# One list scheduler for all engines behind the front, one pool of PSUM banks, and another form of the second layer's seven products

## The chip, the cores and the metric

The kernel runs on one core of a Trainium2 chip. The metric is the device time of one execution in microseconds (us); where several executions were timed, their median stands. A core has a matrix engine (TensorE, PE in the profile, whose weight loads have a row of their own, PEld), VectorE (DVE), ScalarE (ACT), GpSimd (POOL) and SyncE (SP). They run side by side, each takes its own instructions strictly in the order in which the program lists them, and semaphores hold an instruction back until its inputs are there. DMAs that POOL or SP issue run on 16 DMA engines.

## The reference

Chunked attention is followed by two dense layers with a leaky ReLU between them:

```python
q_c, k_c, v_c = (t.reshape(B, H, nc, 64, D) for t in (q, k, v))     # B=8, H=8, S=576, D=64
scores = (1 / sqrt(D)) * matmul(q_c, k_c.transpose(0, 1, 2, 4, 3))  # within chunks of 64 tokens
attn = exp(scores - max(scores)); attn = attn / (sum(attn) + 1e-9)
x = matmul(attn, v_c)                       # as 4608 tokens x 512
h = x @ w_in                                # 512 x 2048
g = maximum(0.01 * h, h)
out = g @ w_out                             # 2048 x 512
```

## The kernel before

**Attention, by groups.** The 4608 tokens are 36 groups of 128 (two chunks of 64). Here a group is called u, from 0 to 35. Its way is: `load_qk` (POOL issues the DMAs that load q and k and cast them to fp16; lines 57 to 77); a transposition of both, by TensorE for the groups 0 to 8 (`stage_tq`, `stage_tk`), by DMA from SP for the later ones (`stage_t`, line 567, tiles QT and KT); `stage_p` on POOL (line 576), which spreads QT into the zero-filled tile QZ; `stage_s` (scores, eight small matmuls on TensorE, line 583, tile Sp); on VectorE and ScalarE the maximum, the subtraction, the exponential, the sum, its reciprocal and the product (lines 593, 598, 605, 612 to 616, 622; tiles mx, sh, ex, z, en); a transposition of the probabilities, by SP's DMA from group 9 on (`stage_d`, line 644, tile et); `stage_v` (eight small matmuls with the values VB, line 657, tile xp); `stage_a` (ScalarE copies xp into xT, line 673). xT is a ring of 1536 tokens. V is loaded for one batch (4.5 groups) at a time into two buffers, `load_v`, line 82.

**The two layers, by blocks.** The tokens are cut into blocks of 128 (six), 256 (one) and 512 (seven, the blocks 7 to 13). The first layer, `mm1` (line 171), makes one PSUM bank at a time, 512 columns of hT, which `act1` (line 191) writes to gT with the leaky ReLU. For the blocks 0 to 6 the second layer is plain (`mm2`, line 203). For the seven large blocks it is one step of a Strassen scheme (`product`, line 298): gT and w_out are each cut in 2 x 2 parts, five sums of gT parts are formed on VectorE (`form`, line 263, tiles S and gT), five sums of weights once (`weight_form`, line 234, tile WF), and seven products of half size replace eight. A product is two passes (p = 0, 1) of eight matmuls of 256 columns. The products go to three banks a, b, c; three ScalarE copies (`evict`) and five VectorE sums (`combine`, lines 334 to 343) turn them into the output tile osb, which SP stores. For the last block the same is done by halves (`piece`).

**What sets the order.** The front, up to the transpositions of q and k of group 5, is a list written by hand (`FRONT`). Behind it a loop over rounds `it` issues the attention of some groups, and `fill` puts pieces of the layers between them: five or six pieces of eight matmuls in a round, picked by `pick` with due times that `on` keeps. A group's scores are issued in one round and its `stage_v` three rounds later. In a round POOL's `stage_p` of group u comes ahead of the load of group u + 7, and SP's transpositions of group u + 3 behind the transposition of the probabilities. The layers use the PSUM banks mm0 to mm3 in turn (three of them from block 7 on); attention has the four banks qp, kp, Sp and ox, of which the products share two.

Of the kernel before, what the change touches and what calls it, by code (L numbers as in the profile page):

```python
# [16 lines left out]
def kernel(  # L17
# [9 lines left out]
    nc = tc.nc  # L27
# [12 lines left out]
    NIN = 9  # L40
# [6 lines left out]
    SUB = {7: 128, **{j: 256 for j in range(8, 14)}}  # L47
    RING = 1536
    HB, HM = NFC // 2, d_model // 2

# [10 lines left out]
    WF = sbp.tile([128, 5, HB, HM], FP16, name="WF")  # L61
# [45 lines left out]
    for eng, name, src in ((nc.sync, "q_f", q), (nc.scalar, "k_f", k)):  # L107
        t = sbp.tile([128, H, D], FP32, name=name, tag=name, bufs=1)
        eng.dma_start(out=t, in_=src[0, :, 0:G, :].rearrange("h p d -> p h d"))
        first.append(t)  # L110
# [8 lines left out]
        "g1 v0 g2 Q0 Q1 g3 Q2 Q3 g4 P0 P1 P2 P3 g5 v1 g6 g7 g8 "  # L119
# [8 lines left out]
    gT: dict[int, bass.AP] = {}  # L128
    GT: dict[int, tuple[int, bass.AP]] = {}

    def tile_of(j):

        return START[j] // 512

    START = [sum(BLOCKS[:j]) for j in range(len(BLOCKS))]
    mm_n = {"n": 0, "of": 4}

    def mm_tile(shape, name):

        i = mm_n["n"] % mm_n["of"]  # L140
        mm_n["n"] += 1
        return psp.tile(shape, FP32, name=name, tag=f"mm{i}", bufs=1)


    T = {"pe": 0.0, "dve": 0.0, "act": 0.0}

    def on(engine, us, after=0.0):
        T[engine] = max(T[engine], after) + us
        return T[engine]

    UNIT = 0.87
    when: dict[tuple, float] = {}

    HT: dict[tuple[int, int, int], bass.AP] = {}
    parts: dict[tuple[int, int], int] = {}
    oP: dict[tuple[int, int], bass.AP] = {}
    made: dict[int, int] = {}
    read = {"tokens": 0}
# [4 lines left out]
    def mm1(j, a, h=0):  # L163
# [3 lines left out]
        hT = mm_tile([128, nf, tb], "hT")  # L167
# [10 lines left out]
        on("pe", UNIT)  # L178
        HT[j, a, h] = hT
        made[j] = made.get(j, 0) + 1  # L180
        if made[j] == NFC * BLOCKS[j] // 512:
            read["tokens"] = START[j] + BLOCKS[j]

    def act1(j, a, h=0):
        tb = sub(j)
        nf = 512 // tb
        n = tile_of(j)
        if n not in GT:
            GT[n] = START[j], sbp.tile([128, NFC, 512], FP16, name="gT", tag="gT", bufs=2)
        gT[j] = GT[n][1][:, :, START[j] - GT[n][0]:START[j] - GT[n][0] + BLOCKS[j]]  # L190
        nc.scalar.activation(  # L191
            out=gT[j][:, nf * a:nf * a + nf, h * tb:h * tb + tb], in_=HT.pop((j, a, h)),
            func=AFT.Prelu, bias=0.0, scale=1.0, alpha=0.01,
        )
        when["gT", j] = on("act", 0.62, T["pe"] + 0.2)

    def mm2(j, ti, part):
        n = parts.get((j, ti), 0)
        if n == 0:
            oP[j, ti] = mm_tile([128, d_model], "oP")  # L200
        o = oP[j, ti]
        for fc in range(part * 4, part * 4 + 4):
            nc.tensor.matmul(  # L203
                out=o,
                lhsT=gT[j][:, fc, ti * 128:(ti + 1) * 128],
                rhs=w_outT[:, fc, :],
                start=(n == 0 and fc == part * 4),
                stop=(n == NFC // 4 - 1 and fc == part * 4 + 3),
            )
        on("pe", UNIT)  # L210
        parts[j, ti] = n + 1

    def store(j, ti):
        osb = sbp.tile([128, d_model], FP32, name="osb", tag="osb", bufs=3, padded_shape=[128, 2 * d_model])
        nc.scalar.activation(out=osb, in_=oP.pop((j, ti)), func=AFT.Copy, bias=0.0, scale=1.0)
        on("act", 0.62, T["pe"] + 0.2)
        r0 = START[j] + ti * 128
        nc.sync.dma_start(out=out[r0:r0 + 128, :], in_=osb)

# [4 lines left out]
    WFORMS = (  # L227
        (B12, B22, ALU.subtract), (B21, B11, ALU.subtract), (B11, B22, ALU.add), (B11, B12, ALU.add),
        (B21, B22, ALU.add),
    )  # L230

    def weight_form(i):
        of, by, op = WFORMS[i]
        nc.vector.tensor_tensor(out=WF[:, i], in0=of, in1=by, op=op)
        on("dve", 1.24)

    SF: dict[int, dict[str, bass.AP]] = {}
    BANK: dict[str, bass.AP] = {}
    TMP: dict[str, bass.AP] = {}
    OSB: dict[tuple[int, int], bass.AP] = {}  # L240

    def half_tokens(j):
        return BLOCKS[j] // 2

    def form(j, name):

        if name in SF.setdefault(j, {}):
            return
        for earlier in FORMS[:FORMS.index(name)]:
            form(j, earlier)  # L250
        g, n = gT[j], half_tokens(j)
        a11, a12 = g[:, :HB, :n], g[:, HB:, :n]
        a21, a22 = g[:, :HB, n:2 * n], g[:, HB:, n:2 * n]
        of, by, op, to = {
            "S2": (a21, a22, ALU.add, None),
            "S1": (a11, a22, ALU.add, None),
            "S5": (a11, a12, ALU.add, None),
            "S6": (a21, a11, ALU.subtract, a21),
            "S7": (a12, a22, ALU.subtract, a12),
        }[name]  # L260
        if to is None:
            to = sbp.tile([128, HB, n], FP16, name=name, tag=name, bufs=1, padded_shape=[128, HB, 256])
        nc.vector.tensor_tensor(out=to, in0=of, in1=by, op=op)  # L263
        SF[j][name] = to
        when[name, j] = on("dve", 0.17 + n / 240, when["gT", j])

    FORMS = ("S2", "S1", "S5", "S6", "S7")
    TAGS = {"a": "qp", "b": "kp", "c": "mm3"}

    LAST = len(BLOCKS) - 1  # L270
    ENDS: dict[tuple[str, int], bass.AP] = {}

    def product(j, m, p):
        g, n = gT[j], half_tokens(j)
        if m not in (3, 4):
            form(j, f"S{m}")
        if m == 3:
            lhs, rhs, bank = g[:, :HB, :n], WF[:, 0], "a"
        elif m == 2:
            lhs, rhs, bank = SF[j]["S2"], B11, "b"  # L280
        elif m == 1:
            lhs, rhs, bank = SF[j]["S1"], WF[:, 2], "c"
        elif m == 4:
            lhs, rhs, bank = g[:, HB:, n:2 * n], WF[:, 1], "b"
        elif m == 5:
            lhs, rhs, bank = SF[j]["S5"], B22, "a"
        elif m == 6:
            lhs, rhs, bank = SF[j]["S6"], WF[:, 3], "c"
        else:
            lhs, rhs, bank = SF[j]["S7"], WF[:, 4], "b"  # L290
        opens = m in (1, 2, 3)
        if opens and j == LAST:
            ENDS[bank, p] = psp.tile([128, HM], FP32, name=f"m{bank}", tag=(TAGS[bank], f"mm{'abc'.index(bank)}")[p], bufs=1)
        elif opens and p == 0:
            mm_n["of"] = 3
            BANK[bank] = psp.tile([128, n // 128, HM], FP32, name=f"m{bank}", tag=TAGS[bank], bufs=1)
# [118 lines left out]
    for j in range(PLAIN):  # L415
        chunks += c1(j) + c2(j)
# [407 lines left out]
```

## Time and profile before

| what | value |
|---|---|
| median of 3 runs | 290.98 us (287.64 to 291.55) |
| span of the profiled execution, its own time | 290.3 us |
| PE busy | 274.7 us, 95% |
| PEld busy | 236.7 us, 82% |
| DVE busy | 202.3 us, 70% |
| ACT busy | 149.4 us, 51% |
| POOL busy | 134.0 us, 46% |
| read and written in HBM | 36.70 and 9.44 MB |

The page tells of one execution: busy time by engine, the span in 40 slices with a digit for the busy share in tenths, the DMA queues, the chain of work that ended last, the costliest groups of instructions, and the DMA issues with the time to their landing. Matmul records overlap: a first-layer matmul of 256 columns is listed with 273 ns, but 24 of them take 2.62 us in the chain. The granted TensorE clock is 1.00 throughout.

### The profile page before, as it was taken

What the parts mean: (1) busy time and instruction counts of PE and PEld (TensorE: products, weight loads), DVE (VectorE), ACT (ScalarE), POOL (GpSimd) and SP (SyncE); (2) the same over time, 40 slices, a digit from 0 to 9 for tenths busy, and PEclk for the clock granted to TensorE, in tenths of its full rate; (3) what the DMA queues carried; (4) which work ended last, traced back from release to release, by engine and by line L of the source; (5) the groups of instructions that cost most, each with busy time, mean ns of one, the idle gap of its engine ahead of it and who ended that gap; (6) DMA issues with size and microseconds to landing.
All of it is one profiled execution on the core that took longest, in us unless ns stands there. A gap on an engine that the chain in (4) does not pass through costs nothing.

```text
span 290.3 us, 7618 instructions
## 1 busy us (share of the span) xinstructions
PE 274.7 (95%) x3188; PEld 236.7 (82%) x3188; DVE 202.3 (70%) x332; ACT 149.4 (51%) x263; POOL 134.0 (46%) x166
## 2 busy tenths in 40 slices
PE   4969999999999989999989699999999999999995
PEld 4859945877859978898869599999899998888884
DVE  6987516798875697868987688879788830820292
ACT  6346724655727736465545455556655554534320
POOL 8846647876496336967643798532150000000000
PEclk9999999999999999999999999999999999999999
DMA  9999999999999999999999999999944201200213
GB/s 131 170 191 172 193 162 197 145 163 169 150 145 163 174 124 130 154 124 187 161 147 156 149 229 164 136 155 179 174 62 125 76 2 65 82 0 2 101 66 126
DMA packets 165795, 39.18 MB, mean 135 GB/s; under 512 B 156800, under 2 KB 161408, under 8 KB 165760
## 3 DMA queue, kind: packets, MB, share of 16 engines
q0 software_dynamic: 114336, 18.09, 91.1%
q1 hardware_dynamic: 50384, 20.33, 43.3%
q8 instruction: 25, 0.41, 0.6%
q10 hardware_dynamic: 1040, 0.26, 0.4%
q14 instruction: 10, 0.08, 0.1%
HBM read 36.70 MB, written 9.44 MB: 159 GB/s over the span
## 4 chain that ended last, share of the span: by engine, by line
PE 51%; DMA 35%; POOL 8%; issue 3%; DVE 1%; ACT 0%; POOLq 0%
PE hT L171 22%; DMA q_in<-in_q_dram 19%; DMA k_in<-in_k_dram 10%; PE mb L298 9%; PE oP L203 6%; PE mc L298 5%; PE ma L298 5%; DMA w_inT<-in_moe_w_in_dram 4%; DMA et<-en 3%; POOL VB L82 3%; POOL QZ L576 2%; POOL k_in L73 2%; PE xp L657 1%; PE Sp L583 1%; POOL q_in L73 1%
## 5 line engine op out<-in xcount | busy, mean ns | idle before, releaser
L171 PE MATMUL hT<-xT,w_inT 128*128 128x256 f16 (+1 forms) x1472 | 143.2, 249 | 1.5 <-DMA w_inT<-in_moe_w_in_dram 1.4
L191 ACT ACTIVATE gT<-hT 128x512 f16<-128x512 f32 x144 | 85.9, 597 | 85.6 <-PE hT L171 84.2
L171 PEld LDWEIGHTS <-w_inT 128*128 128x128 f16 x1472 | 116.9, 98 | 11.6 <-issue 2.0
L576 POOL COPY QZ<-QT 64x512 f16<-64x512 f16 x54 | 42.1, 779 | 21.6 <-DMA QT<-q_in 14.3
L73 POOL DMA_DIRECT2D k_in<-in_k_dram x39 | 32.8, 841 | 31.7 <-DMA VB<-in_v_dram 8.5
L298 PEld LDWEIGHTS <-gT 128*128 128x128 f16 x448 | 42.5, 98 | 4.6
L73 POOL DMA_DIRECT2D q_in<-in_q_dram x39 | 33.1, 849 | 18.6 <-DMA VB<-in_v_dram 8.1
L612 DVE TENSOR_REDUCE z<-ex 128x8 f32<-128x512 f16 x36 | 24.6, 685 | 21.9 <-ACT ex L605 21.7
L298 PEld LDWEIGHTS <-S 128*128 128x128 f16 x336 | 31.7, 98 | 4.3 <-DVE S L263 0.8
L593 DVE TENSOR_REDUCE mx<-Sp 128x8 f32<-128x512 f32 x36 | 24.7, 686 | 12.3 <-PE Sp L583 12.2
L203 PE MATMUL oP<-w_outT,gT 128*128 128x512 f16 x128 | 29.9, 379 | 0.0
L298 PE MATMUL mb<-WF,gT 128*128 128x256 f16 x224 | 28.4, 273 | 0.0
L622 DVE TENSOR_TENSOR en<-ex,zi 128x512 f16<-128x512 f16 x36 | 27.2, 756 | 1.2
L605 ACT ACTIVATE ex<-sh 128x512 f16<-128x512 f32 x36 | 22.5, 625 | 10.3 <-DVE sh L598 10.1
L263 DVE TENSOR_TENSOR S<-gT 128x2048 f16<-128x2048 f16 x21 | 25.4, 1237 | 1.5 <-ACT gT L191 1.5
L598 DVE TENSOR_TENSOR sh<-Sp,mx 128x512 f32<-128x512 f32 x36 | 24.9, 691 | 1.2
L673 ACT ACTIVATE xT<-xp 128x512 f16<-128x512 f32 x36 | 21.3, 593 | 5.7 <-PE xp L657 5.6
L203 PEld LDWEIGHTS <-gT 128*128 128x128 f16 x128 | 11.7, 98 | 11.8
L82 POOL DMA_DIRECT2D VB<-in_v_dram x16 | 18.4, 1157 | 3.6 <-DMA k_in<-in_k_dram 3.0
L583 PEld LDWEIGHTS <-QZ 128*128 128x128 f16 x288 | 12.5, 98 | 7.7 <-POOL QZ L576 5.3
L583 PE MATMUL Sp<-KT,QZ 128*128 128x64 f16 x288 | 14.3, 193 | 4.5 <-POOL QZ L576 3.8
L263 DVE TENSOR_TENSOR gT<-gT 128x2048 f16<-128x2048 f16 x14 | 17.7, 1275 | 0.0
(57 smaller groups left out, 235.0 us busy)
## 6 DMA issues: line engine op xcount, KB each, us to landing
out_dram<-osb SPq DMA_DIRECT2D x12, 512.0 KB, 5.4
VB<-in_v_dram POOLq DMA_DIRECT2D x16, 288.0 KB, 15.0
q_in<-in_q_dram POOLq DMA_DIRECT2D x31, 128.0 KB, 16.5
k_in<-in_k_dram POOLq DMA_DIRECT2D x31, 128.0 KB, 16.8
out_dram<-osb SPq DMA_DIRECT2D x10, 256.0 KB, 6.8
w_inT<-in_moe_w_in_dram POOLq DMA_DIRECT2D x8, 256.0 KB, 9.7
w_outT<-in_moe_w_out_dram POOLq DMA_DIRECT2D x4, 512.0 KB, 9.5
q_in<-in_q_dram POOLq DMA_DIRECT2D x8, 64.0 KB, 11.1
```

The source lines that it names most:

```text
L73: nc.gpsimd.dma_start(out=t[a - r0:z - r0], in_=src[a // S, :, a % S:a % S + z - a, :].rearrange("h p d -> p h d"),)
L82: nc.gpsimd.dma_start(out=VB[b % NVB][m * CH:(m + 1) * CH, :, :, m * CH:(m + 1) * CH].rearrange("p h c d -> p (h c) d"), in_=v[b, m * H // ...
L171: nc.tensor.matmul(out=hT[:, i, :], lhsT=w_inT[:, t, fc * 128:(fc + 1) * 128], rhs=xT[:, t, r0 % RING:r0 % RING + tb], start=(t == 0), sto ...
L191: nc.scalar.activation(out=gT[j][:, nf * a:nf * a + nf, h * tb:h * tb + tb], in_=HT.pop((j, a, h)), func=AFT.Prelu, bias=0.0, scale=1.0, a ...
L203: nc.tensor.matmul(out=o, lhsT=gT[j][:, fc, ti * 128:(ti + 1) * 128], rhs=w_outT[:, fc, :], start=(n == 0 and fc == part * 4), stop=(n == ...
L263: nc.vector.tensor_tensor(out=to, in0=of, in1=by, op=op)
L298: nc.tensor.matmul(out=BANK[bank][:, p, :] if j < LAST else ENDS[bank, p], lhsT=lhs[:, fc, p * 128:(p + 1) * 128], rhs=rhs[:, fc, :], star ...
L576: nc.gpsimd.tensor_copy(out=QZ[u % NQZ][part, :, :, s, :], in_=qt[part])
L583: nc.tensor.matmul(out=Sp[:, i, :], lhsT=qz[:, 2 * m + g, e, :, :], rhs=kt[:, 2 * m + g, e, :], start=True, stop=True)
L593: nc.vector.tensor_reduce(out=MX[u], in_=SP[u], axis=AXL.X, op=ALU.max)
L598: nc.vector.tensor_tensor(out=SH[u], in0=SP.pop(u), in1=MX.pop(u).unsqueeze(2).to_broadcast((128, 8, CH)), op=ALU.subtract)
L622: nc.vector.tensor_tensor(out=E[u], in0=ex, in1=ZI.pop(u).unsqueeze(2).to_broadcast((128, 8, CH)), op=ALU.mult)
```

## The change

Up to the transpositions of q and k of group 5 nothing moves. What comes behind is given to a list scheduler: every operation becomes a `Step` with its engine, a duration, the steps it needs, the PSUM bank or temporary it takes and gives back, a key and, for the scores, an earliest time (5.6 us from one group to the next). `run` takes the step that can begin first by these durations, and writes it into its engine's list. The eight PSUM banks are one pool, and so are seven temporaries. A transposition by DMA is given 1.28 us and 5.0 us to its landing, a load 1.9 us. The q and k tiles have 8 buffers in place of 9 (`NIN`), KT has 4 in place of 6.

The second layer's seven products are another scheme of the same count: four sums of gT and four of w_out, two products that need no sum (1 and 2), and four products (1, 6, 7, 4) that are added up in one PSUM bank, which ScalarE copies out after the first, second, third and fourth. Block 7's first layer works with 256 columns in place of 128. A seven-product form of the first layer is written down too (`first_fast`, `in_product`, `x_form`), but the table `FAST` that would choose blocks for it is empty; its four sums of w_in (`in_form`, tile VF) are made all the same.

The core of the diff:

```diff
-    NIN = 9
+    NIN = 8
-    SUB = {7: 128, **{j: 256 for j in range(8, 14)}}
+    SUB = {j: 256 for j in range(7, 14)}
+    NTMP = 7
+    FAST = {}
-    WF = sbp.tile([128, 5, HB, HM], FP16, name="WF")
+    WF = sbp.tile([128, 4, HB, HM], FP16, name="WF")
+    VF = sbp.tile([128, 4, NT // 2, d_ff // 2], FP16, name="VF")
...
+    def g_form(j, i):
...
+        if i == 0:
+            plus(SF[j, 0], a21, a22)
+        elif i == 1:
+            minus(SF[j, 1], SF[j, 0], a11)
+        elif i == 2:
+            minus(a21, a11, a21)
+        else:
+            minus(a12, a12, SF[j, 1])
...
+    def out_product(j, m, p, tag=None):
...
+            1: (a11, B11), 2: (a12, B21), 3: (a12, B22), 4: (a22, WF[:, 3]), 5: (SF.get((j, 0)), WF[:, 0]),
+            6: (SF.get((j, 1)), WF[:, 1]), 7: (a21, WF[:, 2]),
...
+    LAT = {"pe": 0.25, "act": 0.2, "dve": 0.2, "pool": 0.3, "sp": 3.0, "dma": 1.5}
+    BANKS = ["mm0", "mm1", "mm2", "mm3", "qp", "kp", "ox", "Sp"]
...
+        def begin(s):
+            t = max([now[s.eng], s.at] + [x.end + (x.lat if x.eng != s.eng or x.lat > 1 else LAG[s.eng]) for x in s.after])
...
+        while True:
+            best = None
+            for e in LAT:
...
+                t, s = min((x for x in at if x[0] <= t0 + 0.03), key=lambda x: x[1].key)
+                if best is None or t < best[0]:
+                    best = (t, s)
...
+    def group(u):
+        at = max(0.0, BEGIN + (u - 5) * PACE)
...
+                add(("load", u, i), "pool", 0.86 if (u * G) // S == (u * G + G - 1) // S else 1.7, lambda u=u, i=i: load_half(u, i),
+                    [get(("t", u - NIN, i)) or get(("pe_t", u - NIN, i)), get(("arrive", u - 4, i))], key=5 + u / 100, lat=0.5)
+                add(("arrive", u, i), "dma", 1.9, lambda: None, [get(("load", u, i))], key=u)
...
+                add(("t", u, i), "sp", 1.28, lambda u=u, i=i: stage_t(u, i),
+                    [get(("arrive", u, i)), get(("p", u - 4, 1)), get(("s", u - 4))], key=u, lat=5.0)
+            for s in range(2):
+                add(("p", u, s), "pool", 0.67, lambda u=u, s=s: stage_p(u, s), [get(("t", u, 0)), get(("s", u - NQZ))], key=u / 100)
...
+            add(("s", u), "pe", 0.24, lambda u=u, h=h: stage_s(u, h.slot), need, key=-2, take=[h], at=at)
+            add(("m", u), "dve", 0.61, lambda u=u: stage_m(u), [get(("s", u)), get(("b", u - 2))], key=dve - 6)
...
+            add(("d", u), "sp", 1.28, lambda u=u: stage_d(u), [get(("n", u)), get(("v", u - 4))], key=u, lat=5.0)
...
+        add(("v", u), "pe", 0.24, lambda u=u, h=h: stage_v(u, h.slot), [get(("d", u)) or get(("d2", u)), get(("v_in", b)), get(("v_in", u * G // S))],
+            key=-2, take=[h])
...
+        p1 = mm(1, [g(0, 0)] * 2, spare=SPARE2)
+        d = cp("d", p1)
+        p2 = mm(2, [g(1, 0) + [p1[1]]] * 2)
+        s11 = sum_of("d", 0, lo, [x + osb_free() for x in two(p2, d)], B1)
+        f3 = add(("sf", j, 3), "dve", 1.14, lambda: g_form(j, 3), [f1] + p2, key=6.5 + k0)
+        p6 = mm(6, [[y, f1, wf[1]] for y in (d if last else d * 2)])
+        u2 = cp("u2", p6)
+        p5 = mm(5, [[f0, wf[0], p2[1]]] * 2)
+        p7 = mm(7, [[y, f2, wf[2]] for y in (u2 if last else u2 * 2)])
+        u3 = cp("u3", p7)
+        s22 = sum_of("u3", 1, hi, [x + saves[-2:-1] for x in two(p5, u3)])
+        p4 = mm(4, [[y, wf[3]] + g(1, 1) for y in (u3 if last else u3 * 2)])
+        p3 = mm(3, [[y, f3] for y in (s22 if last else s22 * 2)])
...
+    BEGIN, PACE, SPARE, SPARE2, LEAN, LIMIT = 0.0, 5.6, 1, 0, 0.0, 2
```

More of the change, by code (lines that the diff above doesn't have):

```diff
@@ L206, in mm2 @@
                 rhs=w_outT[:, fc, :],
-                start=(n == 0 and fc == part * 4),
-                stop=(n == NFC // 4 - 1 and fc == part * 4 + 3),
-            )
-        on("pe", UNIT)
-        parts[j, ti] = n + 1
-    def store(j, ti):
[L214 to L218, printed above, removed]
+                start=(fc == 0),
@@ L267, with out_form @@
[L267 to L288, printed above, removed]
[L289 to L296 removed]
+    def out_form(i):
+        if i == 0:
+            minus(WF[:, 0], B12, B11)
+        elif i == 1:
+            minus(WF[:, 1], B22, WF[:, 0])
+        elif i == 2:
+            minus(WF[:, 2], B22, B12)
+        else:
+            minus(WF[:, 3], B21, WF[:, 1])
@@ L793, with __init__ @@
-    fill(len(chunks))
+    for u in range(NIN, UD + 4):
+        load_qk(u)
+    class Hold:
+        def __init__(self, pool):
+            self.pool, self.slot = pool, None
+    class Step:
+        def __init__(self, eng, us, emit, after=(), key=0.0, take=(), give=(), at=0.0, lat=None):
+            self.eng, self.us, self.emit, self.key, self.at = eng, us, emit, key, at
+            self.after = [x for x in after if x is not None]
+            self.take, self.give = take, give
+            self.lat = LAT[eng] if lat is None else lat
+            self.end = None
+            steps.append(self)
```

830 lines of the change are left out of this document (472 added, 358 removed).

## The prediction, made before the changed kernel was run

> **What bounds the kernel now.** I read the page's first two parts, then the three stretches that the trace falls into, then the waits of TensorE.
>
> ```profile
> span 290.3 us, 7618 instructions
> PE 274.7 (95%) x3188; PEld 236.7 (82%) x3188; DVE 202.3 (70%) x332; ACT 149.4 (51%) x263; POOL 134.0 (46%) x166
> ...
> PE   4969999999999989999989699999999999999995
> ...
> DMA  9999999999999999999999999999944201200213
> ...
> 45.10:222.70 177.60, 172.55 (x2033) 147.87 (x2032) 143.97 (x236) 99.58 (x177) 104.73 (x125) 1.00 1.73 155
> 222.70:290.40 67.70, 64.15 (x610) 57.10 (x607) 30.95 (x42) 26.38 (x47) 0.00 (x0) 1.00 0.17 60
> ```
>
> TensorE is the bound. The window rows (length, then busy time of PE, PEld, DVE, ACT, POOL, then clock, DMA share, GB/s) cut the span at the scores of group 5 and of group 35. Attention ends soon after the second cut, and with it the load on the DMA engines: 1.73 before, 0.17 after. To win time the change has to take waits out of the middle, since it does not touch the number of products.
>
> How much is lost there comes from the chain's pieces, which are free of the overlap of matmul records:
>
> ```profile
> 56.51 1.79 PE hT L171 x32
> ...
> 58.97 1.73 PE oP L203 x8
> ...
> 63.78 0.22 PE tpe L631 x4
> ...
> 65.79 0.23 PE xp L657 x8
> ...
> 67.75 0.23 PE Sp L583 x8
> ...
> 247.38 2.62 PE hT L171 x24
> ```
>
> A matmul of 128 columns takes 1.79 / 32 = 0.056 us, of 256 columns 2.62 / 24 = 0.1092, of 512 columns 1.73 / 8 = 0.216, one of the scores or of `stage_v` 0.029, one of a transposition 0.055. The order of before has between the scores of groups 5 and 35 1040 of 256 columns, 384 of 128, 92 of 512, 472 of attention and 44 of transpositions: 113.5 + 21.5 + 19.9 + 13.7 + 2.4 = 171.0 us of work. They took 177.6, so 6.6 us are lost (5.1 of it visible as idle PE). The waits (us in total, how often, the longest) name it:
>
> ```profile
> PEld L583 <- POOL QZ L576: 5.3, 5, 2.5
> ...
> PE Sp L583 <- POOL QZ L576: 3.8, 3, 2.2
> ...
> POOL k_in L73 <- DMA VB<-in_v_dram: 8.5, 3, 5.1
> POOL q_in L73 <- DMA VB<-in_v_dram: 8.1, 5, 2.4
> ...
> PEld L657 <- DMA et<-en: 1.4, 2, 1.0
> ```
>
> The scores wait for POOL's copy into QZ, and that copy stands in POOL's queue behind loads that themselves wait for earlier loads to land.
>
> **The change, part by part.** *The order of attention against the layers* is what matters. In the order of before, every `stage_v` from group 9 on stands 14.7 to 15.4 us of TensorE work behind the scores of its group (for group 24: 128 matmuls of 256 columns and 40 of attention, 14.0 + 1.2 = 15.2). In the new order it stands 11.2 to 16.9 us behind: 11.6 for group 9, 11.7 for 13, 19 and 28, 11.9 for 24 (96 of 256 columns and 48 of attention, 10.5 + 1.4). What the data needs is seen on group 24:
>
> ```profile
> 157.28 0.40 PE L583 MATMUL Sp<-KT,QZ 128*128 128x64 f16 x8
> 157.72 0.69 DVE L593 TENSOR_REDUCE mx<-Sp 128x8 f32<-128x512 f32 x1
> 158.44 0.69 DVE L598 TENSOR_TENSOR sh<-Sp,mx 128x512 f32<-128x512 f32 x1
> 159.96 0.62 ACT L605 ACTIVATE ex<-sh 128x512 f16<-128x512 f32 x1
> 160.61 0.69 DVE L612 TENSOR_REDUCE z<-ex 128x8 f32<-128x512 f16 x1 [1.48 <-ACT ex L605]
> ...
> 162.53 1.35 SPq L644 DMA_TRANSPOSE et<-en  x1
> ...
> 174.84 0.40 PE L657 MATMUL xp<-et,VB 128*128 128x64 f16 x8
> ...
> et<-en SPq DMA_TRANSPOSE x27, 7.9
> ...
> DMA to landing us min/median/max: 2.4/7.9/10.2
> ```
>
> From the scores to the issue of the transposition pass 162.53 - 157.28 = 5.25 us, and the transposition lands 7.9 us after its issue in the median: 13.15 in all. The planner gives it 1.28 + 5.0 = 6.28. With 15.2 us of work between, before had cover for it; with 11.7 TensorE comes to `stage_v` 1.5 us early and stands. A wait moves everything behind it, so only stretches that do not overlap count: groups 9, 13, 19, 24 and 28, 1.55 + 1.45 + 1.45 + 1.25 + 1.45 = 7.2 us of new waits. Lower bound: vector work without any hand-over gap (0.69 + 0.69 + 0.62 + 0.69 in the rows above, and the three short steps behind z, which with z fill the time from 160.61 to 162.53, 1.92) is 0.69 + 0.69 + 0.62 + 1.92 = 3.92, with 7.9 it is 11.8: five times 0.1, nothing. Upper: 5.25 + 10.2 = 15.45, 2.3 more for each, 18.7. I take the median.
>
> Queued behind the waiting `stage_v` is all of TensorE's list, and ScalarE's gT copies wait for that; nothing else is late by it.
>
> ```profile
> QT<-q_in SPq DMA_TRANSPOSE x27, 8.4
> ...
> k_in<-in_k_dram POOLq DMA_DIRECT2D x31, 128.0 KB, 16.8
> ```
>
> The bytes and the number of loads and transpositions are the same as before, on the same queues, so I see no reason for other landing times. The Trainium skill has a rule that speaks against the planner here: "DMA: Bandwidth & Descriptors", section "Issuing engines are not separate DMA queues", says that DMAs of SP, ACT and POOL end on the same 16 engines and interleave. The trace agrees: the transposition lands after 2.4 us at best and 7.9 in the median. The same page, "Latency and other measured facts", gives 261 GB/s for a DMA transposition; by it the 128 KB of et would be an estimated 0.5 us of transfer, and the sum would be that of the fast rival below.
>
> *POOL's and SP's lists.* Each group's QZ copy stands ahead of the loads of group u + 5 or u + 6 instead of behind u + 6, so less of the 3.8 us of waits for QZ comes back; but the scores stand up to 7.3 us earlier in TensorE's work (group 35: 163.5 us of work behind group 5, 171.0 before). Between nothing and the old 3.8 I take half, 1.9. The eighth buffer (nine before) makes a load wait for the transposition one group later; the load waits for landings ahead of it anyway (8.5 and 8.1 us in the rows above): nothing, or what the slow rival costs.
>
> *The sums.*
>
> ```profile
> L263 DVE TENSOR_TENSOR S<-gT 128x2048 f16<-128x2048 f16 x21 | 25.4, 1237 | 1.5 <-ACT gT L191 1.5
> ...
> L263 DVE TENSOR_TENSOR gT<-gT 128x2048 f16<-128x2048 f16 x14 | 17.7, 1275 | 0.0
> ...
> L234 DVE TENSOR_TENSOR WF<-w_outT 128x2048 f16<-128x2048 f16 x5 | 6.1, 1228 | 0.0
> ...
> L343 DVE TENSOR_TENSOR osb<-mb,tt 128x512 f32<-128x512 f32 x6 | 4.1, 685 | 5.7 <-PE mb L298 5.7
> L352 ACT ACTIVATE td<-ma 128x512 f32<-128x512 f32 x6 | 3.5, 587 | 1.2 <-PE ma L298 1.2
> ```
>
> A block loses one gT sum (1.25) and two of five combinations (0.69 each), 2.6 us of VectorE, 18 over seven blocks; three more weight sums (8 for 5, four of which nothing reads) give back 3.7. ScalarE gets one copy of 0.59 per block more. VectorE goes from 202 to about 188 us, ScalarE from 149 to 153: neither is the bound, so the gain is nothing on the path beyond what the lower bound above allows for the chain of attention. New is that the products 1, 6, 7 and 4 share a bank: each waits for ScalarE's copy of the last. The shortest stretch between them in the new order, 7 to 4 in one block, is eight matmuls and a `stage_v`, 0.87 + 0.23 = 1.1 us, against a copy of 0.59 and its two hand-overs; elsewhere it is 1.75 or more. I put it at nothing; with a gT copy ahead of it on ScalarE (0.6) it would be up to 0.5 a block, 3 us.
>
> *Ends.* Block 7 saves 256 x 0.056 - 128 x 0.1092 = 0.3 us. At the last block, product 2 waits for its sum:
>
> ```profile
> 276.40 1.92 PE L298 MATMUL mb<-w_outT,S 128*128 128x256 f16 x16 [0.20 <-DVE S L263]
> ...
> 287.10 0.42 DVE L390 TENSOR_TENSOR osb<-mb,tt 128x256 f32<-128x256 f32 x1 [0.45 <-PE mb L298]
> ```
>
> Products 1 and 2 now need no sum and cover two of them (3.5 us against 2 x 1.24): 0.2 saved. Behind the last matmul the same sum and store stay. The eight banks are the same eight; a gT copy (0.6) still hides behind each piece (0.87).
>
> The sum: 290.3 - 6.6 (old waits) - 0.3 - 0.2 + 7.2 + 1.9 = 292.3 of span. The median of the runs shown, 290.98, is 0.7 above the profiled execution, so 293.0.
>
> **Rivals.** *Fast: no new waits.* If the transposition lands within 6.4 us of its issue, `stage_v` never waits, and the copies into QZ come in time: 290.3 - 7.1 + 0.7 = 283.9. For it: the planner spaces the transpositions, VectorE has 14 us less to do, and the fastest landing is 2.4. Against it: the median under loads is 7.9, and the DMA line reads 9 in every slice up to the thirtieth.
>
> *Slow: loads arrive after their turn.*
>
> ```profile
> 84.36 21.16 DMA q_in<-in_q_dram
> ...
> 118.53 20.78 DMA k_in<-in_k_dram
> ...
> 140.75 20.49 DMA q_in<-in_q_dram
> ```
>
> SP's new list has QT and often KT of group u + 4 ahead of the transposition of the probabilities of group u, where before it had those up to u + 3. By the places in the lists, loads of groups 18, 19, 24 and 29 stand 15.5, 15, 15.5 and 16.6 us of TensorE work ahead of their QT; these three loads took 20.8 in the mean. If POOL issues them no earlier than that, SP stands, et behind it too, and TensorE waits 5.8 (18 and 19 together), 5.3 and 4.2, after 1.55 + 1.45 at groups 9 and 13: 18.3 us. That gives 290.3 - 7.1 + 18.3 + 0.7 = 302.2. It decides from a load of some 17 us on. For it: the three rows. Against it: POOL issues a load as soon as its buffer and the landings ahead allow, which can be earlier than the list's neighbours suggest.
>
> *The change does not do what it says.* The first layer's seven products are not used at all (their table is empty); if the scheduler's order were no better or worse than the old one, its waits would be the old 6.6: 290.98 - 0.5 = 290.5.
>
> **How the numbers follow.** Forecast (waits of some 9 us) 0.42, old waits 0.18, fast rival 0.13, slow rival 0.27. The likeliest gives 293.0. The range reaches to 285 and 302: below lies most of the fast rival, above the worst of the slow one and of the upper bound. Faster or slower by over 2%, about what a measurement of this kernel can tell from no change, means under 285.2 or over 296.8: 0.13 and 0.27; within 0.60.
>
> **What would show it.** Right: in the changed profile TensorE's waits at `stage_v` for et add up to 5 to 10 us, more than those of the scores for QZ; et still lands after some 8 us; the scores of group 35 start some 214 to 220 us into the span, and about 71 us of unbroken work follow; product 2 of the last block does not wait for a sum. Wrong: et lands in 6 us and `stage_v` does not wait (fast rival); or SP waits for q_in or k_in for many us and POOL's loads land later than their turn (slow rival); or TensorE waits for ScalarE's copies within a block, which I put at nothing.

## The result, and the profile after

The changed kernel takes 300.1 us in the median (298.68 to 301.13, four runs), the kernel before 290.31 beside it (287.64 to 291.55): a ratio of 1.035, 95% interval 1.028 to 1.042. It is slower. Ratios, here and below, are formed from the executions in the faster of two states in which a kernel is found, so they need not be the quotient of the medians. The prediction was 293.0, with a range up to 302.0 and a chance of 0.27 for slower by over 2%.

The page of the profiled execution (its own time 298.68 us), parts 1 and 2:

```profile
span 296.9 us, 7334 instructions
PE 276.9 (93%) x3060; PEld 237.2 (80%) x3060; DVE 185.7 (63%) x312; ACT 154.7 (52%) x271; POOL 134.6 (45%) x166
...
PE   4989999996999899988499989999999999999995
...
PEclk9999999998999999999989999999999999999999
```

VectorE has 17 us less to do (14 were worked out), and that brings nothing. The two dents of PE's row, at the digits 6 and 4 (some 74 and 148 us), are the new losses; the clock row dips beside them. The windows, cut at the scores of groups 5 and 35 as before:

```profile
43.90:222.60 178.70, 168.22 (x1839) 141.68 (x1837) 133.77 (x226) 99.84 (x176) 105.31 (x125) 0.98 1.60 151
222.60:296.90 74.30, 71.00 (x674) 63.48 (x672) 24.48 (x31) 31.47 (x56) 0.00 (x0) 1.00 0.18 61
```

The middle holds 7.5 us less of TensorE's work than before and yet takes 178.7 us where it took 177.6. The end, with those 7.5 us added, runs without a loss.

To see where, I take the start of each group's scores and `stage_v` and subtract all TensorE work that stands ahead of it in the order (matmuls at the prediction's 0.056, 0.1092, 0.216, 0.029 and 0.055 us). This delay grows only where TensorE loses time. Between the scores of groups 5 and 35 it grew by 6.2 us in the kernel before (the prediction's 6.6, by a slightly other count) and grows by 14.9 in the changed one. Outside the middle nothing of size changed: span less the delay at group 5 less this growth is 290.3 - 10.7 - 6.2 = 273.4 before and 296.9 - 9.3 - 14.9 = 272.7 after. The jumps of the delay, in order: 0.4 at the scores of group 8, 2.6 at `stage_v` of group 7, 1.2 and 0.8 at the scores of groups 9 and 10, 1.0 at those of 14, then 1.1, 1.1 and 4.05 at `stage_v` of groups 18, 19 and 20, 1.3 at the scores of 23, 0.3 and 1.0 at `stage_v` of 24 and 25. The waits of PE and PEld (in total, how often, the longest) name what ended them:

```profile
PE xp L470 <- DMA et<-en: 6.7, 4, 3.9
...
PE xp L470 <- DVE et L454: 3.2, 2, 2.2
PE Sp L406 <- DMA KT<-k_in: 0.9, 1, 0.9
...
PEld L406 <- POOL QZ L399: 1.1, 1, 1.1
```

The old waits for QZ are nearly gone (the 1.1 and the 0.9 for KT are one moment, at group 14), and waits for et have come. The largest, group 20, in SP's timeline (start, length of the issue):

```profile
134.71 1.88 SPq L393 DMA_TRANSPOSE QT<-q_in  x1
136.69 1.07 SPq L348 DMA_DIRECT2D out_dram<-osb  x2
137.86 2.10 SPq L459 DMA_TRANSPOSE et<-en  x1
140.07 2.86 SPq L393 DMA_TRANSPOSE KT<-k_in  x1
143.03 1.22 SPq L393 DMA_TRANSPOSE QT<-q_in  x1
144.35 2.33 SPq L393 DMA_TRANSPOSE KT<-k_in  x1
```

The probabilities of group 20 are ready at 135.6 us. SP is then issuing QT of group 24 and two stores, so et goes out at 137.86 and lands 9.9 us later. TensorE's timeline shows it (in brackets the idle time before and what ended it), with the other large wait, at group 7:

```profile
70.65 0.39 PE L470 MATMUL xp<-et,VB 128*128 128x64 f16 x8 [2.16 <-DVE et L454]
...
147.84 0.61 PE L470 MATMUL xp<-et,VB 128*128 128x64 f16 x8 [3.89 <-DMA et<-en]
```

Group 7 is still transposed by TensorE, and VectorE copies its et. VectorE's timeline ahead of that copy:

```profile
61.78 1.21 DVE L216 TENSOR_TENSOR WF<-w_outT 128x2048 f16<-128x2048 f16 x1
...
65.50 0.69 DVE L415 TENSOR_REDUCE mx<-Sp 128x8 f32<-128x512 f32 x1
...
67.69 1.21 DVE L216 TENSOR_TENSOR WF<-w_outT,WF 128x2048 f16<-128x2048 f16 x1
...
70.23 0.37 DVE L454 COPY et<-tpe 128x512 f16<-128x512 f16 x1
```

Two of the weight sums that the scheduler put here, and group 8's maximum, stand ahead of work that TensorE waits for. Behind the first wait, and from 0.8 us before the end of the second, the clock is halved for a while (the third last column of the windows):

```profile
71.97:75.39 3.42, 3.42 (x31) 2.68 (x29) 2.19 (x5) 1.19 (x2) 0.55 (x1) 0.50 0.56 105
147.07:150.48 3.41, 2.64 (x19) 2.02 (x20) 0.30 (x1) 0.88 (x2) 1.45 (x2) 0.50 1.63 155
```

TensorE was busy for 3.42 and 2.64 us of them, at half speed, so half of that is lost: 3.0 us, most of the jumps at groups 9, 10 and 23.

Landing times fell, though bytes and counts are the same:

```profile
q_in<-in_q_dram POOLq DMA_DIRECT2D x31, 128.0 KB, 7.1
...
QT<-q_in SPq DMA_TRANSPOSE x27, 6.3
KT<-k_in SPq DMA_TRANSPOSE x27, 5.4
et<-en SPq DMA_TRANSPOSE x27, 5.3
```

A load lands after 7.1 us where it took 16.5, et after 5.3 where it took 7.9. But et is issued later: over the groups 9 to 31 the median from scores to the issue of et rose from 5.7 to 7.4 us, while that from issue to landing fell from 8.3 to 5.7. The later issue has two parts of about the same size: in the mean over these groups the probabilities are ready 6.4 us after the scores where it was 5.6, and then they wait 0.8 us for their turn on SP where it was 0.06.

### The profile page after: what moved, and what is told of

It reads as the page before. It is cut to its first block, busy times and chain, and to the rows that moved or that the text cites. A ratio compares the mean times of both kernels' runs of the same rounds, so it can differ in the third digit from the quotient of the medians.

```text
span 296.9 us, 7334 instructions
## 1 busy us (share of the span) xinstructions
PE 276.9 (93%) x3060; PEld 237.2 (80%) x3060; DVE 185.7 (63%) x312; ACT 154.7 (52%) x271; POOL 134.6 (45%) x166
## 4 chain that ended last, share of the span: by engine, by line
PE 75%; DMA 17%; DVE 3%; POOL 2%; ACT 1%; issue 1%; ACTq 0%; POOLq 0%
PE hT L164 36%; PE oA L336 15%; DMA et<-en 9%; PE oP L189 8%; PE oC L336 7%; DMA w_inT<-in_moe_w_in_dram 6%; PE oB L336 3%; PE xp L470 3%; DMA KT<-k_in 2%; PE Sp L406 2%; POOL VB L86 1%; DVE z L431 1%; DVE en L440 1%; POOL k_in L77 1%; POOL q_in L77 0%
## 5 line engine op out<-in xcount | busy, mean ns | idle before, releaser
L336 PEld LDWEIGHTS <-gT 128*128 128x128 f16 x560 | 53.9, 98 | 6.3
L219 DVE TENSOR_TENSOR osb<-oC,tmp 128x512 f32<-128x512 f32 (+1 forms) x16 | 9.9, 621 | 38.4 <-ACT tmp L177 23.5
L336 PE MATMUL oA<-WF,gT 128*128 128x256 f16 x224 | 28.1, 273 | 0.0
L336 PEld LDWEIGHTS <-S 128*128 128x128 f16 x224 | 22.0, 99 | 2.7
L470 PE MATMUL xp<-et,VB 128*128 128x64 f16 x288 | 14.7, 196 | 10.0 <-DMA et<-en 6.7
L470 PEld LDWEIGHTS <-VB 128*128 128x128 f16 x288 | 12.7, 100 | 12.4 <-DMA et<-en 6.7
L895 POOL DMA_DIRECT2D q_in<-in_q_dram x26 | 21.9, 843 | 0.6 <-PE qp L369 0.6
L895 POOL DMA_DIRECT2D k_in<-in_k_dram x26 | 22.0, 849 | 0.1
L189 PEld LDWEIGHTS <-gT 128*128 128x128 f16 x128 | 11.6, 98 | 11.3
L902 POOL DMA_DIRECT2D VB<-in_v_dram x12 | 13.8, 1156 | 10.2 <-PE xp L470 10.2
L177 ACT ACTIVATE tmp<-oA 128x512 f32<-128x512 f32 (+1 forms) x24 | 13.1, 544 | 10.0 <-PE oA L336 9.8
```

The lines of the kernel that those rows point to most:

```text
L189: nc.tensor.matmul(out=OP[j, ti], lhsT=gT(j)[:, fc, ti * 128:(ti + 1) * 128], rhs=w_outT[:, fc, :], start=(fc == 0), stop=(fc == NFC - 1),)
L336: nc.tensor.matmul(out=to, lhsT=lhs[:, fc, p * 128:(p + 1) * 128], rhs=rhs[:, fc, :], start=(fresh and fc == 0), stop=(fc == HB - 1), skip ...
L470: nc.tensor.matmul(out=xp[:, t, e, :], lhsT=VB[b % NVB][:, t, c, :], rhs=et[:, t // 2, e, t % 2, :], start=True, stop=True,)
L895: nc.gpsimd.dma_start(out=t[a - r0:z - r0], in_=src[a // S, :, a % S:a % S + z - a, :].rearrange("h p d -> p h d"),)
```

## The experiments

Theory at the start: TensorE waits for et because `stage_v` stands too close behind the scores. Rivals: the weight sums hold VectorE up, the pace of the groups is too fast for SP and the DMA engines, SP issues things in the wrong order, or the new products cost something. All in one table; ratios are to the kernel before, each measured beside it (its medians there are 288.9 to 291.0 us). "Lost" is the growth of the delay from group 5 to 35, "a group" the time between those scores divided by 30, the next two columns the medians over groups 9 to 31 from scores to the issue of et and from scores to its landing.

| run | median us | ratio (95%) | span | lost | a group | to issue | to landing |
|---|---|---|---|---|---|---|---|
| before | 290.31 | 1 | 290.3 | 6.2 | 5.92 | 5.7 | 13.9 |
| changed | 300.1 | 1.035 (1.028 to 1.042) | 296.9 | 14.9 | 5.96 | 7.4 | 12.9 |
| e1_lat8 | 296.27 | 1.030 (1.021 to 1.039) | 293.4 | 11.7 | 5.79 | 6.7 | 13.4 |
| e2_lat2 | 324.91 | 1.129 (1.115 to 1.143) | 322.6 | 40.5 | 6.82 | 6.2 | 11.5 |
| e3_sums_later | 300.48 | 1.043 (1.031 to 1.054) | 298.3 | 16.0 | 6.00 | 6.9 | 14.1 |
| e4_both | 296.2 | 1.030 (1.022 to 1.037) | 293.7 | 11.1 | 5.77 | 7.5 | 14.8 |
| e5_scheme_alone | 289.14 | 1.001 (0.997 to 1.005) | 288.8 | 6.4 | 5.92 | 5.7 | 13.4 |
| e6_et_first | 294.54 | 1.019 (1.008 to 1.031) | 295.5 | 13.1 | 5.83 | 7.0 | 13.8 |
| e7_pace62 | 289.8 | 1.003 (0.997 to 1.008) | 286.7 | 4.8 | 6.12 | 5.8 | 13.0 |
| e8_pace62_et_first | 289.6 | 1.003 (0.998 to 1.008) | 287.4 | 5.4 | 6.14 | 5.9 | 13.4 |
| e9_pace_alone | 293.76 | 1.013 (1.002 to 1.024) | 291.7 | 9.0 | 6.35 | 5.5 | 11.5 |
| e10_qt_early | 293.97 | 1.013 (1.005 to 1.021) | 291.9 | 9.5 | 6.28 | 6.4 | 13.4 |
| e11_scheme_p_ahead | 287.19 | 0.987 (0.982 to 0.991) | 285.7 | 3.3 | 5.82 | 5.8 | 13.9 |
| e12_p_ahead_old_products | 288.01 | 0.991 (0.986 to 0.995) | 285.5 | 2.5 | 5.80 | 5.8 | 14.3 |

In every row the span is 272.7 to 273.4 us, plus 9.0 to 9.9 of delay at group 5 (10.7 in before), plus what is lost. So what follows is all about that one column.

**The cover, more and less of it.** The planner's time for et's landing in the changed kernel:

```
-            add(("d", u), "sp", ..., key=u, lat=5.0)
+            add(("d", u), "sp", ..., key=u, lat=8.0)      # e1_lat8
+            add(("d", u), "sp", ..., key=u, lat=2.0)      # e2_lat2
```

> One number of the planner is changed: it counts 8.0 us in place of 5.0 from the issue of the transposition of the probabilities (et) to its landing, so that stage_v stands 14.2 us of TensorE work or more behind the scores of its group (11.2 to 16.9 in the changed kernel). Theory, values too early: the waits of stage_v for et from group 9 on (7.6 us between the groups 18 and 25 of the changed kernel) go, and with the longest of them the second stretch at half clock; the first stretch, before group 9, stays: 290 to 293 us. Rival, et late by its own queue: the 4 us wait of group 20 comes from two stores that stand ahead of et on SP, and it stays: 296 to 299 us.

> The same number set the other way, 2.0 us: stage_v stands 8.3 to 13.2 us of work behind its scores. Theory, values too early: by the 13.2 us that the data takes, some 19 groups wait, about 37 us in all, 30 more than in the changed kernel: 325 to 335 us. Rival, only single hiccups count: 300 to 308 us.

Taking cover away costs about what the theory says (324.9 us, at the low end of its range), in another mix: nine waits for et of 26.4 us in all where it had some 19 of about 37, and 23.9 us of the span at half clock. The row of e2_lat2:

```profile
PE xp L470 <- DMA et<-en: 26.4, 9, 7.4
```

Giving it (at least 14.2 us of work between scores and `stage_v`) brought less than expected. In the time it cannot be told apart from the changed kernel (1.030 against 1.035, intervals that overlap), and in the trace 3.2 of the 14.9 us went. Now et takes 13.4 us to land instead of 12.9 and uses part of the added cover up; the waits for it fall from 7.6 to 4.4 us in the jumps. And a wait has come that the changed kernel does not have: `stage_v` stands later, xT is there later, and the first layer waits for it at 88.6 us:

```profile
PE hT L164 <- ACT xT L482: 2.1, 1, 2.1
```

With a stretch at half clock behind it this costs 4.0 us. So the cover is a cause, and not all of it, and more of it has a price.

**The weight sums.** Out go the four sums that nothing reads, and the four WF sums come later:

```
-        add(("wf", q_), "dve", ..., at=12.0 + 3 * q_)
-    for q_ in range(4):
-        add(("vf", q_), "dve", ..., at=12.0 + 15 + 3 * q_)
+        add(("wf", q_), "dve", ..., at=34.0 + 4 * q_)
```

> The four sums of w_in that nothing reads are left out, and the four sums of w_out may begin 34 us behind the front in place of 12, so that none stands in VectorE's list among the work of the groups 6 to 9. Theory, sums in the way: the 3 us that TensorE waits at groups 7 and 8 and the first stretch at half clock (1.7 to 2 us) go: 294 to 296 us. Rival, the waits only move to the next group whose values come too early: 298 to 301 us.

> Both edits, 8.0 us for et and the weight sums later, the four unread sums left out. If the two causes are separate they add up: 300.1 - 7.6 - 1.3 - 5 = 286 us, 285 to 288, faster than the kernel before. If a common limit lies behind them (the landing of loads and transpositions), it shows as waits of the scores for QZ or KT and the time stays at 291 or above.

The wait at group 7 fell from 2.6 to 1.2 us, and with it the half clock behind it went. But the later groups then waited more, and 16.0 us were lost in all: the rival of e3_sums_later. The wait was real and not what set the end. e4_both added nothing to the longer cover alone either. Its SP timeline shows where it stands:

```profile
158.88 2.00 SPq L459 DMA_TRANSPOSE et<-en  x1
160.99 2.60 SPq L393 DMA_TRANSPOSE QT<-q_in  x1
163.69 1.25 SPq L393 DMA_TRANSPOSE KT<-k_in  x1
165.05 0.52 SPq L348 DMA_DIRECT2D out_dram<-osb  x1
165.66 1.35 SPq L459 DMA_TRANSPOSE et<-en  x1
```

SP has no idle time here. The probabilities of group 25 were ready at 161.5 us, and their transposition had to wait for QT, KT and a store until 165.66. From this came two new theories: SP's order, or the rate.

**Order against rate.** Four kernels, the two edits of e4_both with each combination of these:

```
-                    [get(("arrive", u, i)), get(("p", u - 4, 1)), get(("s", u - 4))], ...
+                    [get(("arrive", u, i)), get(("p", u - 4, 1)), get(("n", u - 4))], ...   # et first
-    BEGIN, PACE, ... = 0.0, 5.6, ...
+    BEGIN, PACE, ... = 0.0, 6.2, ...                                                        # pace 6.2
```

> The kernel with both edits of e4_both (296.2 us), and in addition the transpositions QT and KT of group u wait for en of group u - 4 instead of its scores, so that on SP they stand behind the transposition of et of group u - 4, as in the kernel before. TensorE's order keeps at least 13.1 us of work between scores and values. Theory (et stands late because SP issues QT, KT and stores ahead of it): from scores to issue of et falls from 7.5 to 5.7 to 6.3 us in the median, the landing stays at some 8, so 13.5 to 14.2 in the sum; TensorE's waits for et fall from some 9 to 3 to 5 us; 290 to 292 us. Rival (the 16 DMA engines are the limit and whatever is issued earlier lands as much later): from scores to landing stays at 14.5 to 15 us, the time at 295 to 297.

> The kernel with both edits of e4_both (296.2 us), and in addition PACE 6.2 instead of 5.6: the scores of a group are due every 6.2 us, so group 35's stand 213 us into TensorE's work instead of some 196. Theory (SP's order holds et up): SP has 10% more room, from scores to issue of et falls only a little, 7.5 to 6.8 us; 292 to 295 us. Rival (the rate of transfers is the limit: at 5.6 us a group SP and the DMA engines have no room left, at the pace of before, some 5.9, they just had): from scores to landing falls from 14.8 to 12.5 to 13.5 us, few waits for et stay, 288 to 291 us.

> Both of the two edits before this one: PACE 6.2, and QT and KT of group u behind en of group u - 4, with the longer time for et's landing in the planner and the later weight sums. Theory (order on SP): as with the order alone, 289 to 292 us, the pace adding at most 1 us. Rival (rate): as with the pace alone, 288 to 291, the order adding at most 1 us. If both matter by themselves, 285 to 288, below the kernel before, from scores to landing at 12 to 13 us and hardly a wait for et left.

The rate decides. At pace 6.2 the loss falls from 11.1 to 4.8 us and the ratio from 1.030 to 1.003 (intervals apart). The order on SP brings about 1% at pace 5.6, with intervals that overlap (its trace is of an execution of 297.3 us, 2.8 above its median, and shows no smaller loss), and nothing at 6.2, so no effect of its own is shown. The windows of e7_pace62:

```profile
43.80:227.30 183.50, 179.49 (x1975) 153.50 (x1973) 132.80 (x225) 105.21 (x186) 102.30 (x125) 1.00 1.62 153
227.30:286.70 59.40, 56.15 (x538) 50.17 (x536) 19.30 (x29) 25.55 (x46) 0.00 (x0) 1.00 0.17 59
```

and its waits:

```profile
PE hT L164 <- ACT xT L482: 2.4, 3, 1.2
PE tpe L448 <- DVE en L440: 1.1, 3, 0.7
PE xp L470 <- DVE et L454: 0.8, 1, 0.8
PE Sp L406 <- DMA KT<-k_in: 0.7, 1, 0.7
```

No wait for et's landing is left, and the clock is 1.00. Half of what is still lost is the first row: the first layer waits for xT, as in e1_lat8. Group 35 comes 4.7 us later than in the changed kernel, and the end is 14.9 us shorter (59.4 instead of 74.3): TensorE does the layers' work while attention catches up, instead of waiting and doing it at the end. From scores to landing it fell from 14.8 to 13.0 us, as the rival of e7_pace62 has it, and most of that lies ahead of the issue (7.5 to 5.8).

**The pace alone**, in the changed kernel, with the short cover and the early sums left in:

```
-    BEGIN, PACE, ... = 0.0, 5.6, ...
+    BEGIN, PACE, ... = 0.0, 6.2, ...
```

> The changed kernel (300.1 us) with one edit: PACE 6.2 instead of 5.6. The planner's time for et's landing stays at 5.0 and the weight sums stay where they are, so that fourteen of the stage_v stand under 13.2 us of work behind their scores (11.2 to 12.6). Theory (the pace of the groups is the cause by itself: at 5.6 us a group SP's list and the DMA engines have no room, whatever the cover): from scores to landing of et falls from 12.9 to 12 us or less, waits for et to some 4 us, 290 to 293 us. Rival (the cover is a cause of its own: stage_v too close behind the scores): with the 13.0 us that e7_pace62 showed from scores to landing, the new order has some 13 us of waits for et, 296 to 299 us.

The one number brings the ratio from 1.035 to 1.013, 2.2% (intervals apart), where the longer cover alone gave 0.5%, and et lands 11.5 us behind the scores. The median is 0.8 over what the theory gave and 2.2 below the rival. What it keeps is what the theory left in:

```profile
PE xp L470 <- DMA et<-en: 3.8, 4, 1.6
...
PE xp L470 <- DVE et L454: 2.7, 2, 2.2
```

These, and up to 1.7 us of half clock behind the wait of 2.2, come to more than the waits for xT and KT (2.4 and 0.7 us in e7_pace62) that it is spared.

**QT and KT earlier**, on top of e7_pace62:

```
-                    [get(("arrive", u, i)), get(("p", u - 4, 1)), get(("s", u - 4))], ...
+                    [get(("arrive", u, i)), get(("p", u - 5, 1)), get(("s", u - 6))], ...   # QT, KT: bufs=6
```

> The kernel of e7_pace62 (289.8 us), with QT and KT in six buffers each instead of four and allowed from the scores of group u - 6 on instead of u - 4; the tables that nothing reads (VF, XF) are not allocated, which makes the room. What e7_pace62 still lost between the scores of groups 5 and 35 were 2.0 and 1.4 us at the scores of groups 13 and 16, whose QT was issued 10 and 14 us ahead of them because on SP it stood behind an et that waited for its en. Theory (SP's one list is the last of the loss): QT of groups 13 and 16 is issued earlier and those 3.4 us go, 285 to 287.5 us, below the kernel before. Rival (earlier QT and KT put themselves ahead of et on SP, as in e4_both, and load the DMA engines earlier): et is issued later, 6.5 us or more behind the scores, and waits for et come back, 290 to 293 us.

The rival was right in the main (294.0 us where it had 290 to 293, the issue 6.4 us behind the scores where it had 6.5 or more). QT of group 13 came no earlier (82.9 us, 82.5 in e7_pace62), and the next ones put themselves ahead of et, as at group 19, whose probabilities were ready at 135.5 us:

```profile
135.40 0.54 SPq L347 DMA_DIRECT2D out_dram<-osb  x1
136.04 1.85 SPq L392 DMA_TRANSPOSE QT<-q_in  x1
137.99 0.90 SPq L347 DMA_DIRECT2D out_dram<-osb  x1
138.97 1.33 SPq L458 DMA_TRANSPOSE et<-en  x1
```

```profile
147.64 0.46 PE L469 MATMUL xp<-et,VB 128*128 128x64 f16 x8 [1.95 <-DMA et<-en]
```

This wait was followed by another stretch at half clock. The theory had misplaced the loss, too: of the 3.4 us that it gave to QT, TensorE idled 0.98 and 1.22 in e7_pace62 ahead of the first layer, for xT, and 0.67 for KT.

**The products alone**, in the old rounds:

```
-    ORDER = (3, 2, 1, 5, 4, 6, 7)
+    ORDER = (1, 2, 6, 5, 7, 4, 3)
-            "S2": (a21, a22, ALU.add, None),  ... S1, S5, S6, S7
+            "S5": (a21, a22, ALU.add, None),
+            "S6": (SF.get(j, {}).get("S5"), a11, ALU.subtract, None),
+            "S7": (a11, a21, ALU.subtract, a21),
+            "S3": (a12, SF.get(j, {}).get("S6"), ALU.subtract, a12),
...    # banks, copies, additions and weight sums as in the changed kernel
```

> The kernel before with only the second layer's products exchanged: products in the order 1, 2, 6, 5, 7, 4, 3 with four sums of activations, four weight sums, three outputs' additions and four copies a block; the rounds, the places of attention, the banks' names and the loads are those of before. Theory (the whole loss of the change lies in where the scheduler puts attention, and the products cost what they cost before): within 1% of before, 287 to 291 us, with the old waits for QZ (some 6 us) and no wait of TensorE for a copy of bank A over 0.3 us. Rival (products 1, 6, 7 and 4 in one bank wait for ScalarE's copies, 0.3 to 0.5 us a block or more): 292 to 296 us, and the waits of TensorE have rows at the products' line released by the copies of bank A.

The ratio is 1.001 (0.997 to 1.005): the new products neither cost nor bring anything by themselves. Its waits:

```profile
PE Sp L563 <- POOL QZ L556: 3.6, 2, 2.2
PE xp L637 <- DMA et<-en: 1.5, 1, 1.5
PE xp L637 <- DVE et L618: 0.8, 1, 0.8
PE ma L287 <- ACT tu L336: 0.5, 1, 0.5
```

The first three are those of before, with 0.8 us more for et's landing. The last is the copy of bank A, which the prediction put at nothing with up to 3 us as its bound; it costs 0.5 us, once.

**A version that beats both.** The old waits for QZ can be taken out without a scheduler:

```
-        if UD <= it < NU:
-            stage_p(it)
+        if UD <= it + 1 < NU:
+            stage_p(it + 1)
```

> The kernel of e5_scheme_alone (the rounds of before with the new products, 289.1 us) with one more edit: stage_p(it + 1) instead of stage_p(it), so that POOL's copy into QZ of a group stands one round (5.7 us) earlier in POOL's list, ahead of the loads that hold it up. Theory (the waits that the old order had are only those of the scores for POOL's copy, and it is late by the loads ahead of it): the waits of the scores for QZ (4.4 us) go, nothing else is late, 284 to 286 us. Rival (the copy now waits on POOL for QT's landing or for the scores of three groups earlier, and the loads behind it come later): loads and QT land later, waits for KT or et take the place, 288 to 292 us.

> The kernel before with one edit, stage_p(it + 1) instead of stage_p(it), and its own old products: e11_scheme_p_ahead (ratio 0.987) without the change's products. Theory (the products are neutral with or without the old waits; what e11 won is POOL's earlier copy alone): ratio 0.982 to 0.992, 285.5 to 288.5 us, with 2 us of waits for QZ at most. Rival (the new products' 18 us less of VectorE's sums show only where the waits for QZ are gone; e5_scheme_alone could not show it): ratio 0.994 to 1.0, 289 to 291 us, with waits of TensorE for sums of activations or for en's transposition in their place.

With the new products the ratio is 0.987 (0.982 to 0.991), with the old ones 0.991 (0.986 to 0.995): the same within their intervals, so the products are neutral here too, and the win is POOL's copy. In e11_scheme_p_ahead no wait for QZ is left:

```profile
PE xp L637 <- DVE et L618: 1.1, 1, 1.1
PE xp L637 <- DMA et<-en: 0.9, 1, 0.9
PE ma L287 <- DVE S L261: 0.7, 1, 0.7
PE ma L287 <- ACT tu L336: 0.5, 1, 0.5
```

The gain of 0.9 to 1.3% is less than the 2% that theory set for e11_scheme_p_ahead: 3.3 us remain lost, in small waits.

## Why the prediction was right or wrong

**Right.** TensorE is the bound, and the time is decided between the scores of groups 5 and 35. The old waits for QZ go. New waits at `stage_v` for et come in their place: 7.2 us predicted, 7.6 in the jumps (1.1 + 1.1 + 4.05 + 0.3 + 1.0). The way from scores to landing, put at 13.15 us, was 12.9, by two errors that cancel (below). The sums, the copies of bank A, the pool of banks and the last block cost nothing on the path: product 2 of the last block does not wait, behind group 35 nothing is lost, and e5_scheme_alone and e12_p_ahead_old_products confirm that the products are neutral in the old rounds.

**The step that failed: the sum's terms for the middle.** I had 7.2 + 1.9 = 9.1 us of waits, and there are 14.9.

- QZ: 1.9 set, 1.0 seen, at the scores of group 14, where KT landed at the same moment (99.0 us).
- Half clock: not in the sum, 3.0 us (in the jumps of 1.2, 0.8 and 1.3).
- VectorE's copy of et at group 7: not in the sum, 2.6 us. I costed the weight sums by VectorE's busy total, "neither is the bound", and did not ask what stands behind them in VectorE's list. As e3_sums_later shows, this term does not set the end by itself.

With 7.6 for et and 0.7 in small ones these make the 14.9. That 300.1 us lies inside the range is luck in part: the upper end, 302, was drawn from the slow rival and from longer waits for et, and neither came. What filled the gap had been put at nothing.

**The size was right for the wrong reason.** The 7.6 us are not the five equal waits at groups 9, 13, 19, 24 and 28 that I had. Groups 9, 13 and 28 did not wait, 19 and 24 waited 1.1 and 0.3 us, and the rest came at 18, 25 and above all 20 (1.1, 1.0 and 4.05), whose et landed 17.9 us behind its scores. I took 5.25 us to the issue and 7.9 to the landing as properties of the data, since "the bytes and the number of loads and transpositions are the same". Both were properties of the old order. In the new order the loads land in 7.1 us and et in 5.3, and et is issued later, half because the probabilities are ready later and half because SP's list has QT, KT and stores ahead of it. The prediction noted that the scores come up to 7.3 us earlier in TensorE's work, and used it only for QZ. That was the cause: 163.5 us of work for 30 groups is 5.45 us a group, where the old order had 5.7, and the chip delivered a group every 5.96 us. At 6.2, with more cover and the sums later (e7_pace62), the loss falls to 4.8 us, below that of before, with the same scheduler and the same products; e9_pace_alone shows that the pace alone does most of it.

**The rivals.** The slow rival gave 302.2 us, near what was measured, by another mechanism: loads late for their turn on SP. That fell: no long wait of SP for a load is in the trace. The fast rival asked for et within 6.4 us of its issue; the median did land sooner, and TensorE waited all the same, because the issue had moved. Old waits unchanged: fell.

**Ends.** The scores of group 35 start at 222.6 us, predicted 214 to 220. Outside the middle the two traces differ by 2.1 us: 0.7 at the end (273.4 - 272.7), of which 0.5 stood in the sum, and 1.4 ahead of group 5 (10.7 - 9.3), which did not. The 1.4 is no gain of the change: every other row of the table has 9.0 to 9.9, those with the old order too, and in the profiled execution of before TensorE waited 1.4 us for w_in in the front. The median lies 3.2 us above the profiled span, where 0.7 had been added: 1.8 in the execution itself, 1.4 between it and the median. By the same 1.8 the profiled execution of before took an estimated 292.1 us, above its median; so the spans differ by 6.6 us and the medians by 9.8.

**What stays open.** What limits the rate. Transpositions take 110 us of SP's issue time in the changed kernel and 122 in e4_both (81 of 1.36 and 1.50 us), of the 171 and 165 us over which they are spread; their landing depends on the load, too. Which of the two binds was not separated. That no kernel here took under 5.77 us a group points to a limit of that size; it is argued, not shown. Nor is the pace all of it. The old rounds with POOL's earlier copy (e11_scheme_p_ahead, e12_p_ahead_old_products) plan 5.70 us of work a group, attain 5.82 and 5.80, and lose only 3.3 and 2.5 us; there every `stage_v` from group 9 on has 14.7 us of cover or more. Whether the scheduler would do as well at 5.7, or with that cover, was not tried.

## What to carry to other kernels

A list scheduler's planned pace is a claim on every queue behind it: before trusting it, divide the planned work by the number of stages and compare with the rate that the old trace attained (here 5.45 us planned, 5.92 attained, and 5.80 once the waits for QZ were out), since an in-order engine that runs ahead of its data only waits, and the work it could have done meanwhile stands at the end. Times from issue to landing belong to an order and its load, not to a transfer, so a changed order needs a range for both the issue and the landing, and a wait taken out upstream may only bring the next one forward. Total busy time of an engine that is not the bound says nothing about which of its instructions stand in front of one that TensorE waits for.

## What the runs showed of the hardware

Short idle stretches of TensorE can halve its clock. The clock stood at 0.5 for 3.41 us behind idle stretches of 2.16 (changed kernel), 2.17 (e9_pace_alone) and 1.95 us (e10_qt_early), and within and behind one of 3.89 (changed kernel), which costs up to 1.7 us each time. The length fits the Trainium skill, "TensorE: Matmul & The Clock Gate", section "Part 1: The HAM clock gate (the "warmup" mystery)", which gives a free-running window of 3413 ns. The Trainium skill speaks there of an idle window of about that length as the cause; here idle times of about 2 us were enough, though not always. In e1_lat8 TensorE idled for 2.49 us,

```profile
175.40 0.41 PE L470 MATMUL xp<-et,VB 128*128 128x64 f16 x8 [2.49 <-DMA et<-en]
```

and kept its clock over the window (third last column 1.00):

```profile
172.90:180.00 7.10, 4.61 (x55) 4.19 (x55) 4.75 (x8) 2.52 (x5) 2.42 (x4) 1.00 1.61 171
```

What decides can be read from the fourteen traces together. In each, all changes of the clock lie on one grid of 3.413 us, which cuts the trace into cells from the first change to the end. Sixteen of the 1162 cells of these grids hold 1.95 us or more in which TensorE was idle, and the cell behind each of them is at half clock. No cell with 1.94 us or less has such a cell behind it, but for one in e2_lat2 that was at half clock itself. The 2.15 us ahead of 88.6 us in e1_lat8 lie in one cell, and the clock halved; the 2.49 us shown above are cut by the edge of a cell into 1.56 and 0.93. The ends of matmuls are modelled in a trace, so the bound of some 1.9 us is rough.

So a wait of 2 us may cost 2 or almost 4, by how it lies on a grid that begins at another place in each execution (its first edge is 0.0 to 3.3 us behind the start of the span).
